# The fifteen multiplications of attention output by broadcast reciprocals, on GpSimd instead of VectorE

## The chip, the cores and the metric

The kernel runs on one core of a Trainium2 chip. Its time is device microseconds of one execution. Three runs of the kernel before gave 645.48, 646.23 and 646.55 us; the median is 646.23 us.

## The reference

Two blocks read the same input x (1 x 2048 x 512, bf16) and are mixed by a gate:

```
g = sigmoid((x * gate_w).sum(-1, keepdims=True))
qkv = x @ wqkv                       # 32 heads of 16
p = softmax(q @ k^T * 16 ** -0.5)
a = (p @ v) @ wo
b = ((x @ w_gate) * (x @ w_up)) @ w_down      # F = 1376
out = g * a + (1 - g) * b
```

## The kernel before, in words

**Tiling.** The 2048 queries are cut into four chunks of 512 (`cq`). The attention runs in 32 steps `m` (`NG`), eight for each chunk; a step covers four heads, one in each 32-row group of TensorE. Two steps, p = 0 and p = 1, make a pair `cb = m // 2` of eight heads, and a pair's result fills block `b` of the attention output OT of its chunk, so there are sixteen pairs. For each step TensorE multiplies a head's keys and queries into a PSUM bank (scores, L910, 128 keys x 512 queries, four heads side by side), and later exponentials and values into one bank (L1143, bank `OB`, the value bank), where a column of ones beside the values sums the denominators.

**Exponentials.** Two engines make them out of the score banks. ScalarE takes most tiles with its exponential (L1008, one to three banks at a time). VectorE takes the others with an approximation (L1043): it adds a bias and writes 16-bit integers whose bits are read as fp16. GpSimd then adds two constants to those bits, four 16-bit numbers at a time as a 64-bit integer (L1093, INT64_ADD), which makes two shifted copies; TensorE multiplies all three into the values, the copies with values scaled to match (VS). Results lie in the 58 cells of PT.

**Normalising a pair.** When a step's products are done, VectorE copies the value bank to `oc` (L1240, fp32). The denominators of both steps go through a DMA to `dn`, VectorE takes reciprocals (L1231) and multiplies them by the gate (L1229), DMAs write them to DRAM (L1228) and read them back broadcast over partitions into `rb` (L1224), and four DMAs bring the odd heads' rows into place in `oc` (L1196). Then comes the instruction that the change moves: L1222 multiplies `oc` by `rb`, both 128 x 512 fp32 in SBUF, into OT (bf16). Fifteen of the sixteen pairs go this way; the last has a path of its own (L1213 and after L1246). The next pair's first copy into `oc` (L1240) and its load of `rb` wait for that product (`mult_done`), and so do the output projections that read the block (`ev_ot`, L427 and L433).

**Order.** The program is recorded before it is built. A planner (`_Clock`) plays the kernel through with booked durations and picks, for each engine, the next ready task; a string of digits (`ORDER`) settles its choices. Each pick is appended to one list, and `emit` deals that list out to the engines: an engine's instructions stand in the order of the list, and a wait on a semaphore is set for each dependency on another engine's result or a DMA. Every engine runs its own list strictly in order. `eng` says which engine an operation goes to; `stream` and `seq` say which count the waits use.

```
o = K.issue("pool", fn, [x[2] for x in us] + [d for z in zs for d in pt_rel[z]], 157.0 + 218.0 * n, 182.0 + 218.0 * n)
...
const("pool", "add0", lambda g: g.int64_add(dmy[:, :].bitcast(I64), dmy[:, :].bitcast(I64), 0), ["dmy", "wgz", "qz0"], 1500, 1500)
```

The first line books an add, two of which follow each VectorE exponential; the second is a dummy add at the start (L416, booked at 1500 ns) whose result nobody reads.

Beside the attention run the projections of q, k and v, the up, gate and down products of the second block and the output projections, as fillers on TensorE (L427), with VectorE taking their results out of PSUM (L489, L534, L555, L624, L651, L714).

## Time and profile before

| | |
|---|---|
| median of three runs | 646.23 us |
| profiled execution, time | 647.98 us |
| profiled execution, span of the core | 645.3 us |
| granted TensorE clock | 1.0 |
| TensorE busy | 638.4 us, 99% |
| ScalarE busy | 622.0 us, 96% |
| VectorE busy | 605.1 us, 94% |
| GpSimd busy | 554.1 us, 86% |

A row of the costliest groups reads: line, engine, operation, what it writes and reads, shapes, count, then busy time and the mean duration of one, then the engine's idle time ahead of them and what ended it. A row of the timeline reads: start, duration, engine, line, operation, count merged, and in brackets the idle time ahead and what ended it. DVE is VectorE, ACT ScalarE, POOL GpSimd, PE TensorE, PEld its weight loads, SP the engine that issues DMAs. A q behind an engine's name stands for its sequencer.

### The profile page before, as it was taken

Reading aid. Unit: us, or ns where it says so; the run is one execution under the profiler, and the core shown is the slowest. Engines: PE = TensorE matmul, PEld = TensorE weight load, DVE = VectorE, ACT = ScalarE, POOL = GpSimd, SP = SyncE. Lnnn points to the kernel's source line nnn. Section 1 sums busy time; section 2 is a strip of 40 time slices with the busy share of each in tenths; the row PEclk is TensorE's granted clock in tenths of the full one; section 3 lists DMA queues with packets and bytes.
Section 4 is the critical chain, followed back from the end, with each engine's and each line's share of the span. In section 5 each row is a group of like instructions: output and inputs, shape, how many; then the busy total and the mean of one; then the engine's idle time right before and its main releaser. Section 6 shows DMA issues by size and latency. Waiting matters only on the chain.

```text
span 645.3 us, 21200 instructions
## 1 busy us (share of the span) xinstructions
PE 638.4 (99%) x8733; PEld 192.2 (30%) x8733; DVE 605.1 (94%) x1021; ACT 622.0 (96%) x753; POOL 554.1 (86%) x1431
## 2 busy tenths in 40 slices
PE   8999999999999999999999999999999999999997
PEld 3332332232223222223322222332322222322233
DVE  6999999999999999999998999999998999999986
ACT  5899999999999999999999999999999999999993
POOL 2669899998998989898889999988898998899982
PEclk9999999999999999999999999999999999999999
DMA  7940101000010100101010010100001010000101
GB/s 151 266 120 16 66 10 40 2 16 24 4 35 10 40 14 16 32 1 35 5 30 16 16 40 11 31 8 12 27 6 40 19 35 3 8 24 1 28 20 35
DMA packets 28658, 21.15 MB, mean 33 GB/s; under 512 B 16488, under 2 KB 24396, under 8 KB 28560
## 3 DMA queue, kind: packets, MB, share of 16 engines
q1 hardware_dynamic: 27600, 19.26, 11.6%
q8 instruction: 68, 1.11, 0.7%
q10 hardware_dynamic: 960, 0.52, 0.3%
q14 instruction: 30, 0.25, 0.1%
HBM read 11.63 MB, written 2.37 MB: 22 GB/s over the span
## 4 chain that ended last, share of the span: by engine, by line
PE 88%; ACT 9%; DVE 1%; DMA 1%; issue 0%; SPq 0%
PE ps L1143 32%; PE ps L427 28%; PE ps L910 26%; ACT PT L1008 9%; PE ps L433 3%; DVE OT L1222 1%; DMA wq<-in_A_wqkv_dram 1%; DVE PT L1043 0%; PE ps L1254 0%; SPq L354 0%; DVE QE L714 0%; PE ps L1446 0%; DVE fl L1441 0%; DVE cb L1451 0%
## 5 line engine op out<-in xcount | busy, mean ns | idle before, releaser
L1008 ACT ACTIVATE PT<-ps 128x1024 bf16<-128x1024 f32 (+2 forms) x743 | 616.2, 1001 | 6.6 <-PE ps L910 5.8
L1093 POOL INT64_ADD PT<-PT x1420 | 551.2, 413 | 76.2 <-DVE PT L1043 67.6
L1043 DVE TENSOR_SCALAR PT<-ps 128x512 int16<-128x512 f32 x728 | 471.5, 683 | 26.9 <-PE ps L910 15.5
L910 PE MATMUL ps<-QE,KK 32*128 32x512 bf16 x2048 | 245.7, 384 | 0.6 <-DVE PT L1043 0.4
L1143 PE MATMUL ps<-PT,V 128*32 128x512 bf16 (+1 forms) x2048 | 232.5, 384 | 0.0
L1143 PE MATMUL ps<-PT,VS 128*32 128x512 f16 x1456 | 186.7, 383 | 0.0
L910 PEld LDWEIGHTS ps<-QE,KK 32*128 32x128 bf16 x2048 | 63.7, 91 | 231.1 <-ACT PT L1008 183.7
L1143 PEld LDWEIGHTS ps<-PT,V 128*32 128x32 bf16 x2048 | 57.7, 95 | 62.9 <-issue 49.4
L1143 PEld LDWEIGHTS ps<-PT,VS 128*32 128x32 bf16 x1456 | 45.6, 95 | 42.0 <-issue 26.8
L427 PE MATMUL ps<-xT,wg 128*32 128x512 bf16 x704 | 54.6, 383 | 0.7 <-DVE PT L1043 0.7
L427 PE MATMUL ps<-xT,wu 128*32 128x512 bf16 x704 | 54.1, 383 | 0.0
L427 PE MATMUL ps<-wd,wa 128*32 128x512 bf16 x704 | 51.6, 382 | 0.0
L624 DVE TENSOR_TENSOR usb<-ps,omg 128x512 bf16<-128x512 f32 x44 | 29.9, 680 | 0.2
L651 DVE TENSOR_TENSOR wa<-ps,usb 128x512 bf16<-128x512 f32 x44 | 29.9, 680 | 0.1
L433 PE MATMUL ps<-wo,OT 32*128 32x512 bf16 x60 | 23.1, 385 | 0.1
L1240 DVE COPY oc<-ps 128x512 f32<-128x512 f32 x31 | 21.1, 680 | 0.0
L427 PEld LDWEIGHTS ps<-wd,wa 128*32 128x32 bf16 x704 | 14.8, 95 | 19.5 <-issue 11.9
L427 PE MATMUL ps<-xT,wa 128*32 128x512 bf16 x272 | 20.2, 382 | 0.0
L427 PEld LDWEIGHTS ps<-xT,wg 128*32 128x32 bf16 x704 | 13.8, 95 | 19.5 <-issue 11.1
L427 PEld LDWEIGHTS ps<-xT,wu 128*32 128x32 bf16 x704 | 13.8, 95 | 18.9 <-issue 10.4
L427 PE MATMUL ps<-xT,wq 128*32 128x512 bf16 x256 | 18.5, 382 | 0.6 <-DMA wq<-in_A_wqkv_dram 0.6
L427 PE MATMUL ps<-wa,xT 128*32 128x512 bf16 x256 | 17.1, 381 | 0.0
(74 smaller groups left out, 145.4 us busy)
## 6 DMA issues: line engine op xcount, KB each, us to landing
rb<-rscr SPq DMA_DIRECT2D x16, 256.0 KB
QE<-Qr SPq DMA_DIRECT2D x120, 16.0 KB, 1.8
oc<-oc SPq DMA_DIRECT2D x60, 32.0 KB, 1.9
out_dram<-ost SPq DMA_DIRECT2D x12, 128.0 KB, 1.8
wu<-in_B_w_up_dram SPq DMA_DIRECT2D x1, 1376.0 KB, 7.2
wg<-in_B_w_gate_dram SPq DMA_DIRECT2D x1, 1376.0 KB, 11.5
wd<-in_B_w_down_dram SPq DMA_DIRECT2D x1, 1280.0 KB, 14.9
wa<-in_A_wqkv_dram SPq DMA_DIRECT2D x1, 512.0 KB, 6.1
```

What stands on the lines that cost most here:

```text
L427: r = pe.matmul(ps[32 * i : 32 * i + 32, bank, :], w, x_, start=s0, stop=s1, tile_position=(0, 32 * i), skip_group_check=True)
L433: return pe.matmul(ps[:, bank, :], lhs[32 * q : 32 * q + 32, :], rhs[32 * q : 32 * q + 32, :], start=s0, stop=s1, tile_position=(32 * q, 0 ...
L624: return v.tensor_tensor(usb[:, st["s"], :], ps[:, bank, :], omg[:, cf, :], ALU.mult)
L651: return v.tensor_tensor(hT[:, f, :], ps[:, bank, :], usb[:, u_at[cf, f][0], :], ALU.mult)
L910: return lambda pe: pe.matmul(ps[:, bank, :], KK[32 * j : 32 * j + 32, b, kt * 128 : (kt + 1) * 128], QE[32 * j : 32 * j + 32, p, b, :], s ...
L1008: o = K.issue("act", lambda a: a.activation(PT[:, cs, :], ps[:, bs, :], ACT.Exp, scale=math.log(2.0) / 1024.0), deps, 63.0 + 427.0 * n, 17 ...
L1043: o = K.issue("dve", lambda v: v.tensor_scalar(PT[:, y, :].bitcast(I16), ps[:, bank, :], BIAS16, 0.0, ALU.add, ALU.max), [dep] + pt_rel[y] ...
L1093: return g.int64_add(PT[:, zl, :].bitcast(I64), PT[:, sl, :].bitcast(I64), w)
L1143: return lambda pe: pe.matmul(ps[32 * it.j : 32 * it.j + 32, OB, :], lhs, it.rhs, start=s0, stop=s1, tile_position=(0, 32 * it.j), skip_gr ...
L1222: lambda v: v.tensor_tensor(OT[:, cq % 2, b, :], oc[:, 0, :], rb[:, :], ALU.mult), 760.0, 840.0, None, 1, begun=md)
L1240: K.task("dve", deps, lambda v: v.tensor_copy(oc[:, p, :], ps[:, OB, :]), 600.0, 690.0, done, 0)
```

## The change

When the planner has picked a pair's multiplication and booked it on VectorE, the recorded operation is relabelled: its engine and stream become GpSimd's, and the two counters are put right. The planner still books VectorE's time for it, so no other choice moves: the whole list keeps its order, and fifteen entries of it go to another engine.

```diff
                                     def md(o7):
+                                        P.nstream["dve"] -= 1
+                                        o7.eng = o7.stream = "pool"
+                                        P.nstream["pool"] = o7.seq = P.nstream["pool"] + 1
                                         for tt in range(4):
                                             ev_ot[cq, b, tt] = o7
                                         mult_done[cb] = o7
```

Lines behind the diff move down by three: L1222 becomes L1225, L1240 becomes L1243.

GpSimd's list at the first of the fifteen places, the change against before (a + is new; names are the tiles written and read, PT the exponentials' cells, OT the attention output, oc the copied value bank, rb the broadcast reciprocals; s_dve, s_pe, s_drb and s_dodd are the semaphores of VectorE, TensorE, the load of rb and the moves of odd rows):

```order
 L1093 ISA PT<-PT 128x256 [waits s_dve]
 L1093 ISA PT<-PT 128x256
+L1225 ISA
+L1225 TENSOR_TENSOR OT<-oc,rb 128x512 [waits s_drb,s_dodd]
+L1093 ISA
 L1093 ISA PT<-PT 128x256 [waits s_dve,s_pe]
 L1093 ISA PT<-PT 128x256
```

Three instructions have come in between two pairs of adds: the multiplication, and one without operands on either side of it. In the built program these two are PseudoReloadLibraryIndex, the first with library index 0, the second with 1. Before, the program holds a single one, with index 1, ahead of the dummy add of L416. The same three stand at all fifteen places.

VectorE's list at the same place, from the last exponentials ahead of the multiplication to the copy of the next step's value bank, before:

```order
L1043 TENSOR_SCALAR PT<-ps 128x512 [waits s_pe] x2
L1222 TENSOR_TENSOR OT<-oc,rb 128x512 [waits s_drb,s_dodd]
L1043 TENSOR_SCALAR PT<-ps 128x512 [waits s_pe]
L489 CAST KK<-ps 128x512 [waits s_pe]
L1043 TENSOR_SCALAR PT<-ps 128x512 [waits s_pe] x2
L1043 TENSOR_SCALAR PT<-ps 128x512
L1043 TENSOR_SCALAR PT<-ps 128x512 [waits s_pe]
L1240 COPY oc<-ps 128x512 [waits s_pe]
```

and after:

```order
L1043 TENSOR_SCALAR PT<-ps 128x512 [waits s_pe] x3
L489 CAST KK<-ps 128x512 [waits s_pe]
L1043 TENSOR_SCALAR PT<-ps 128x512 [waits s_pe] x2
L1043 TENSOR_SCALAR PT<-ps 128x512
L1043 TENSOR_SCALAR PT<-ps 128x512 [waits s_pe]
L1243 COPY oc<-ps 128x512 [waits s_pool,s_pe]
```

The multiplication and its two DMA waits are gone from VectorE, nothing else has changed places, and the copy at the end, which overwrites `oc`, has a wait for GpSimd in addition.

## The prediction

> **What bounds the kernel now.** I read the page first: shares of busy time, then the costliest groups.

> ```profile
> span 645.3 us, 21200 instructions
> ...
> PE 638.4 (99%) x8733; PEld 192.2 (30%) x8733; DVE 605.1 (94%) x1021; ACT 622.0 (96%) x753; POOL 554.1 (86%) x1431
> ...
> L1008 ACT ACTIVATE PT<-ps 128x1024 bf16<-128x1024 f32 (+2 forms) x743 | 616.2, 1001 | 6.6 <-PE ps L910 5.8
> L1093 POOL INT64_ADD PT<-PT x1420 | 551.2, 413 | 76.2 <-DVE PT L1043 67.6
> L1043 DVE TENSOR_SCALAR PT<-ps 128x512 int16<-128x512 f32 x728 | 471.5, 683 | 26.9 <-PE ps L910 15.5
> ```

> ScalarE's exponentials alone fill 616 of 645 us, with 6.6 us of idle time ahead of them. TensorE waits for the score banks that they empty (the waits, below). VectorE and GpSimd form a second chain: VectorE writes an approximate exponential (L1043), GpSimd makes two shifted copies of it (L1093), TensorE multiplies all three into the values. That chain has little room left. The stretch from the first to the last multiplication, and its waits:

> ```profile
> core 0: us, PE busy (x) PEld busy (x) DVE busy (x) ACT busy (x) POOL busy (x), PEclk, DMA share, GB/s
> 76.00:612.00 536.00, 534.51 (x7280) 156.05 (x7280) 512.34 (x833) 533.70 (x634) 484.94 (x1249) 1.00 0.07 19
> ```

> ```profile
> PEld ps L910 <- ACT PT L1008: 183.7, 439, 0.5
> ...
> PEld ps L1143 <- POOL PT L1093: 7.3, 32, 0.2
> ```

> ACT is idle for 536.00 - 533.70 = 2.3 us there, and GpSimd for 536.00 - 484.94 = 51.1 us. These two numbers decide: VectorE time that is set free can shorten the kernel by hardly more than the 2.3 us, and GpSimd can take on about 51 us more, or 3.4 us for each of fifteen steps, before it sets the pace itself. Tensor work waits for an add only 32 times and never over 0.2 us: the adds now come early.

> **Part 1: what leaves VectorE.**

> ```profile
> L1222 DVE TENSOR_TENSOR OT<-oc,rb x15: 672/727/1906, 77.2 to 609.6; 128x512 bf16<-128x512 f32 x15
> ```

> ```profile
> L1222 DVE TENSOR_TENSOR OT<-oc,rb 128x512 bf16<-128x512 f32 x15 | 14.3, 951 | 0.0
> ```

> Fifteen instructions of 0.67 to 1.91 us, 14.3 us together, leave VectorE. Three are near 1.8 us, and here is what happens at one of them (VectorE, GpSimd, ScalarE):

> ```profile
> 148.77 1.91 POOL L1093 INT64_ADD PT<-PT  x5
> ...
> 149.32 1.91 DVE L1222 TENSOR_TENSOR OT<-oc,rb 128x512 bf16<-128x512 f32 x1
> ...
> 151.15 0.68 DVE L1043 TENSOR_SCALAR PT<-ps 128x512 int16<-128x512 f32 x1
> ...
> 151.93 0.77 POOL L1093 INT64_ADD PT<-PT  x2 [1.24 <-DVE PT L1043]
> ...
> 152.91 1.02 ACT L1008 ACTIVATE PT<-ps 128x1024 bf16<-128x1024 f32 x1 [0.72 <-PE ps L910]
> ```

> The multiplication ends 0.55 us after GpSimd's run of adds does (151.23 against 150.68): it could not get through while the adds ran back to back. ScalarE then stands for 0.72 us. The other two long ones cost it 0.40 and 0.18 us:

> ```profile
> 227.92 1.02 ACT L1008 ACTIVATE PT<-ps 128x1024 bf16<-128x1024 f32 x1 [0.40 <-PE ps L910]
> ```

> ```profile
> 536.37 1.02 ACT L1008 ACTIVATE PT<-ps 128x1024 bf16<-128x1024 f32 x1 [0.18 <-PE ps L910]
> ```

> Moving the multiplication ends these, since VectorE's work next to it reads PSUM: a gain of 0.72 + 0.40 + 0.18 = 1.3 us on the path. The rest of the 14.3 us is covered by ScalarE, which is busy all the while. Where the multiplication goes through at once, an add beside it stretches, as at the second one:

> ```profile
> L1093 POOL INT64_ADD PT<-PT x5: 394/402/830, 110.9 to 112.9; - x5
> ```

> That gives GpSimd back 0.83 - 0.40 = 0.4 us a time.

> **Part 2: what comes to GpSimd.** The order shows three new instructions at each of the fifteen places: a reload of GpSimd's instruction library (the program's PseudoReloadLibraryIndex, 0), the multiplication, and a second reload (1) ahead of the next add. The diff does not say so; adds and multiplication belong to different libraries. All three stand in line with the adds, so nothing of them is hidden except by GpSimd's own idle time.

> The multiplication itself: no two-input GpSimd operation stands in the trace. Bounds are the fill below, 1.38 us for 1536 numbers, so 0.46 us for 512, and four times an add of 0.40 us (an add reads 256 words, the multiplication 1024), 1.6 us. I take the middle, 1.0 us; the ends move the total by 15 x 0.6 = 9 us at most.

> The reload: the trace has one, ahead of the dummy add that the program makes early on.

> ```profile
> 4.14 1.38 POOL L415 MEMSET QE<- 128x1536 f32 x1 [2.19 <-DVE sel L406]
> 5.67 0.19 POOL L416 INT64_ADD dmy<-dmy  x1
> 13.33 0.78 POOL L1093 INT64_ADD PT<-PT  x2 [7.47 <-DVE PT L1043]
> ```

> ```profile
> L416 POOLq MODIFY_POOL_CONFIG  x2: 12/12/12, 5.5 to 5.6; - x2
> ```

> From the end of the fill (5.52) to the add (5.67) are 0.15 us: the lower end. The upper end is what GpSimd's idle time of 7.47 us behind it could have hidden, 7.5 us. Between them I have to choose. Nothing in the program before ever goes back to library 0, and the profiled execution is one of several of this program, so that one reload may have found its library already in place; after the change all thirty really switch. The planner also books 1500 ns for the dummy add, not the 192 ns that it took here. If code has to come from DRAM, the nearest rows are the single fetches of the start:

> ```profile
> wa<-in_A_wqkv_dram SPq DMA_DIRECT2D x1, 512.0 KB, 6.1
> ...
> wq<-in_A_wqkv_dram SPq DMA_DIRECT2D x1, 128.0 KB, 4.9
> ```

> I take the middle of these, 5.5 us, as an estimate. The sum for each place is 2 x 5.5 + 1.0 - 0.4 = 11.6 us, for fifteen 174 us; GpSimd's idle time takes up 51 of that, and 123 us are left. TensorE's early adds do not help for long: once it has used those made before a stall, each of its shifted products waits for GpSimd, scores stop, and ScalarE with them. The profiled execution took 648.0 us (a span of 645.3 and 2.7 around it), 1.7 more than the median of 646.2. From the median: 646.2 + 123 = 769 us; the 1.3 us of part 1 vanish in it.

> [...]

> **Part 3: waits that move.** VectorE loses its wait for the reciprocals' and the odd rows' DMAs (s_drb, s_dodd); GpSimd gets it, with all later adds behind it. It never held VectorE (idle 0.0 in the multiplication's row), and GpSimd reaches the place about when VectorE did, because an add follows its VectorE exponential closely. With 5.5 us of reload ahead, the data is there. VectorE's next copy out of the value bank (L1240, L1243 after) now waits for GpSimd; behind it are queued VectorE's exponentials, and TensorE waits for the bank:

> ```profile
> 77.19 0.73 DVE L1222 TENSOR_TENSOR OT<-oc,rb 128x512 bf16<-128x512 f32 x1
> ...
> 81.86 0.68 DVE L1240 COPY oc<-ps 128x512 f32<-128x512 f32 x1
> ```

> The copy starts 3.9 us after the multiplication's end. With 5.5 + 1.0 us on GpSimd against 0.73 it would stand for about 2 us, but inside the 11.6 us that the adds are held anyway, so I add nothing; with a cheap reload it costs nothing. The other reader is the output projection. At one place it follows at once:

> ```profile
> 492.51 0.68 DVE L1222 TENSOR_TENSOR OT<-oc,rb 128x512 bf16<-128x512 f32 x1
> ...
> 493.63 0.39 PE L427 MATMUL ps<-wo,OT 128*32 128x512 bf16 x4
> ```

> There TensorE, 0.4 us behind the product, waits from the first reload on, about 1 us if the reload is free and 6 us as forecast, again inside the 11.6. rb is loaded again a head pair later, and SP's order stays as it is: both at nothing.

> **Rivals.**

> *The reload finds both libraries in place* (not slower): then it is worth the 0.15 us of the dummy's row, fifteen places cost 15 x (0.3 + 1.0 - 0.4) = 13.5 us of 51 idle ones, and the three gains of 1.3 us remain, less what late adds and that one projection cost. 646.2 - 1.3 = 644.9 at best; if one place in three has no room and loses 0.9 us, 649. I say 645.5. For it: the row. It decides as long as 15 x (2c + 0.6) stays below 51 us, so for a reload c up to 1.4 us. Against it: that row needs no switch to have happened. Chance 0.31: 0.10 faster, 0.16 the same, 0.05 slower.

> *The reload costs about what ScalarE's table load does.*

> ```profile
> L386 ACT ACT_TABLE_LOAD x1 | 1.3, 1283 | 2.2 <-issue 2.2
> ```

> With 1.28 us, fifteen places cost 15 x 3.16 = 47 us, just under the 51 idle ones on average; but each is a block of 3.2 us, and places with less room let TensorE stand for part of it, at most about 20 us altogether: 650 to 665 us. Chance 0.12, slower.

> *VectorE is the bound and the reload is free*: its 14.3 us all come off, 632 us. Against it: ACT's 2.3 us of idle time. Chance 0.02, faster.

> **How the numbers follow.** My forecast, the reload as a fetch, has 0.55 and is the likeliest: 769 us, all of it slower. Its own range runs from 3.0 us a reload, 15 x 6.6 - 51 = 48 us, 694 us, to 7.5 us, 15 x 15.6 - 51 = 183 us, 829 us. A fast reload holds 0.33, too much to leave out, so the range starts at 645 and is cut at 815, leaving out the best cases below and the dearest above, some 15 in 100. A measurement of this kernel can tell a change of about 0.2%, 1.3 us. Faster: 0.10 + 0.02 = 0.12; the same: 0.16; slower: 0.55 + 0.12 + 0.05 = 0.72.

> **What would show it.** In the changed profile: thirty more library rows on GpSimd, and behind each a gap or a long first instruction of about 5.5 us; the multiplication at about 1.0 us; adds without the 0.8 us ones; ACT with idle time behind TensorE in fifteen places 38 us apart, and TensorE's value products waiting for GpSimd in long waits instead of 0.2 us. I am wrong if the adds follow the reload within 0.5 us and GpSimd's busy share only rises to some 88%; then the time stays within 3 us of before. I am wrong about the idle time if the reload is as forecast but much less than 51 us, or more, is given back.

## The result and the profile after

The median after is 836.52 us (six runs, 833.63 to 838.91), against 646.35 us for six runs of the kernel before on the same chip: a ratio of 1.2947, interval 1.293 to 1.2965, or 190 us more. (The ratios in this document can differ from the quotient of the two medians by up to 0.0008.) The direction was as forecast. The size was not: 769 us was the forecast, and 815 the end of the range.

The profiled execution took 836.67 us. From its page, the same lines as the prediction shows of the kernel before, and the moved multiplication's row:

```profile
span 833.6 us, 21266 instructions
...
PE 690.1 (83%) x8733; PEld 197.4 (24%) x8733; DVE 598.9 (72%) x1006; ACT 629.2 (75%) x753; POOL 564.5 (68%) x1446
...
L1008 ACT ACTIVATE PT<-ps 128x1024 bf16<-128x1024 f32 (+2 forms) x743 | 623.4, 978 | 187.6 <-PE ps L910 186.0
L1093 POOL INT64_ADD PT<-PT x1420 | 542.7, 400 | 148.3 <-DVE PT L1043 74.0
L1043 DVE TENSOR_SCALAR PT<-ps 128x512 int16<-128x512 f32 x728 | 474.2, 685 | 140.3 <-PE ps L910 130.1
...
L1225 POOL TENSOR_TENSOR OT<-oc,rb 128x512 bf16<-128x512 f32 x15 | 18.8, 1252 | 105.9 <-issue 99.0
```

The loss can be read off ScalarE: its exponentials' idle time has gone from 6.6 to 187.6 us, 181.0 more, and their busy time from 616.2 to 623.4, 7.2 more. Together that is 188.2 us, and the span has grown by 833.6 - 645.3 = 188.3 us. GpSimd's busy share has fallen from 86 to 68%: no engine is full any more. The waits, sorted by size:

```profile
ACT PT L1008 <- PE ps L910: 186.0, 67, 13.9
PEld ps L910 <- ACT PT L1008: 170.2, 396, 0.8
DVE PT L1043 <- PE ps L910: 130.1, 123, 14.2
PEld ps L1143 <- POOL PT L1093: 127.7, 84, 13.1
POOL OT L1225 <- issue: 99.0, 14, 7.6
PE ps L1143 <- POOL PT L1093: 96.9, 18, 12.8
...
POOL PT L1093 <- issue: 64.5, 11, 6.0
...
DVE oc L1243 <- POOL OT L1225: 26.8, 7, 6.1
```

TensorE's value products now wait for an add for up to 13.1 us, where the longest such wait was 0.2 us. GpSimd itself waits for nothing that has a name ("issue"): 99.0 / 14 = 7.1 us ahead of a multiplication, 64.5 / 11 = 5.9 us ahead of the next add. These are the two reloads. In the instruction list they are hardly to be seen: the sequencer's rows of one source line last 1 to 13 ns each, with a median of 11.

```profile
L1225 POOLq MODIFY_POOL_CONFIG  x30: 1/11/13, 77.7 to 783.0; - x30
```

The first of the fifteen places, GpSimd's timeline and then ScalarE's:

```profile
76.95 0.77 POOL L1093 INT64_ADD PT<-PT  x2 [0.29 <-DVE PT L1043]
84.67 1.25 POOL L1225 TENSOR_TENSOR OT<-oc,rb 128x512 bf16<-128x512 f32 x1 [6.95 <-issue]
91.98 32.14 POOL L1093 INT64_ADD PT<-PT  x86 [6.06 <-PE ps L910]
```

```profile
69.28 15.19 ACT L1008 ACTIVATE PT<-ps 128x1024 bf16<-128x1024 f32 x16
88.01 1.02 ACT L1008 ACTIVATE PT<-ps 128x1024 bf16<-128x1024 f32 x1 [3.54 <-PE ps L910]
89.96 2.08 ACT L1008 ACTIVATE PT<-ps 128x512 bf16<-128x512 f32 x3 [0.92 <-PE ps L910]
94.04 1.02 ACT L1008 ACTIVATE PT<-ps 128x1024 bf16<-128x1024 f32 x1 [2.01 <-PE ps L910]
```

No add is made from 77.72 to 91.98 us, a block of 14.3 us. ScalarE works on for 6.8 us, to 84.47, then stands for more than half of the time until the block's end, and again behind it. Over the fifteen places GpSimd's mean idle time is 105.9 / 15 = 7.06 us ahead of a multiplication and 5.86 us behind it, so a block is 7.06 + 1.25 + 5.86 = 14.17 us. The loss, 190.2 / 15 = 12.7 us for each place, is nearly all of it.

### The profile page after: what moved, and what is told of

Its sections match the earlier page's. It is cut to its first block, busy times and chain, and to the rows that moved or that the text cites. A ratio compares the mean times of both kernels' runs of the same rounds, so it can differ in the third digit from the quotient of the medians.

```text
span 833.6 us, 21266 instructions
## 1 busy us (share of the span) xinstructions
PE 690.1 (83%) x8733; PEld 197.4 (24%) x8733; DVE 598.9 (72%) x1006; ACT 629.2 (75%) x753; POOL 564.5 (68%) x1446
## 2 busy tenths in 40 slices
DMA packets 28659, 21.16 MB, mean 25 GB/s; under 512 B 16488, under 2 KB 24396, under 8 KB 28560
## 4 chain that ended last, share of the span: by engine, by line
PE 52%; POOL 20%; issue 19%; DVE 8%; DMA 1%; SPq 0%; POOLq 0%; DVEq 0%
PE ps L1143 18%; POOL PT L1093 18%; PE ps L427 17%; PE ps L910 15%; DVE PT L1043 5%; POOL OT L1225 2%; PE ps L433 2%; DVE oc L1243 1%; DVE usb L624 1%; DMA wq<-in_A_wqkv_dram 1%; DVE rec L1232 0%; DVE wa L651 0%; DVE Qr L534 0%; DVE rec L1234 0%; DVE ost L714 0%
## 5 line engine op out<-in xcount | busy, mean ns | idle before, releaser
L1008 ACT ACTIVATE PT<-ps 128x1024 bf16<-128x1024 f32 (+2 forms) x743 | 623.4, 978 | 187.6 <-PE ps L910 186.0
L1093 POOL INT64_ADD PT<-PT x1420 | 542.7, 400 | 148.3 <-DVE PT L1043 74.0
L1043 DVE TENSOR_SCALAR PT<-ps 128x512 int16<-128x512 f32 x728 | 474.2, 685 | 140.3 <-PE ps L910 130.1
L1143 PE MATMUL ps<-PT,VS 128*32 128x512 f16 x1456 | 212.2, 399 | 99.2 <-POOL PT L1093 96.9
L1143 PE MATMUL ps<-PT,V 128*32 128x512 bf16 (+1 forms) x2048 | 244.0, 399 | 21.1 <-DVE oc L1243 21.1
L910 PE MATMUL ps<-QE,KK 32*128 32x512 bf16 x2048 | 253.8, 399 | 3.1 <-DVE PT L1043 3.0
L910 PEld LDWEIGHTS ps<-QE,KK 32*128 32x128 bf16 x2048 | 63.1, 91 | 241.2 <-ACT PT L1008 170.2
L1225 POOL TENSOR_TENSOR OT<-oc,rb 128x512 bf16<-128x512 f32 x15 | 18.8, 1252 | 105.9 <-issue 99.0
L1143 PEld LDWEIGHTS ps<-PT,VS 128*32 128x32 bf16 x1456 | 50.2, 95 | 164.4 <-POOL PT L1093 127.7
L1143 PEld LDWEIGHTS ps<-PT,V 128*32 128x32 bf16 x2048 | 59.0, 96 | 88.3 <-issue 53.5
L1243 DVE COPY oc<-ps 128x512 f32<-128x512 f32 x31 | 21.2, 685 | 63.8 <-PE ps L1143 37.0
L427 PE MATMUL ps<-xT,wu 128*32 128x512 bf16 x704 | 56.7, 400 | 1.7 <-DVE PT L1043 1.7
L427 PE MATMUL ps<-xT,wg 128*32 128x512 bf16 x704 | 57.4, 401 | 0.0
L427 PE MATMUL ps<-wd,wa 128*32 128x512 bf16 x704 | 55.9, 410 | 0.0
L427 PE MATMUL ps<-wo,OT 128*32 128x512 bf16 x196 | 17.1, 395 | 12.9 <-POOL OT L1225 12.9
L427 PE MATMUL ps<-xT,wa 128*32 128x512 bf16 x272 | 20.8, 392 | 0.0
L427 PEld LDWEIGHTS ps<-wd,wa 128*32 128x32 bf16 x704 | 15.3, 98 | 22.2 <-issue 15.2
L427 PEld LDWEIGHTS ps<-xT,wu 128*32 128x32 bf16 x704 | 14.2, 97 | 23.5 <-issue 13.0
L427 PEld LDWEIGHTS ps<-xT,wg 128*32 128x32 bf16 x704 | 14.3, 96 | 20.7 <-issue 14.1
## 6 DMA issues: line engine op xcount, KB each, us to landing
out_dram<-ost SPq DMA_DIRECT2D x12, 128.0 KB, 1.7
wg<-in_B_w_gate_dram SPq DMA_DIRECT2D x1, 1376.0 KB, 11.5
wa<-in_A_wqkv_dram SPq DMA_DIRECT2D x1, 512.0 KB, 6.2
```

The costliest lines, as they stand in the source:

```text
L427: r = pe.matmul(ps[32 * i : 32 * i + 32, bank, :], w, x_, start=s0, stop=s1, tile_position=(0, 32 * i), skip_group_check=True)
L910: return lambda pe: pe.matmul(ps[:, bank, :], KK[32 * j : 32 * j + 32, b, kt * 128 : (kt + 1) * 128], QE[32 * j : 32 * j + 32, p, b, :], s ...
L1008: o = K.issue("act", lambda a: a.activation(PT[:, cs, :], ps[:, bs, :], ACT.Exp, scale=math.log(2.0) / 1024.0), deps, 63.0 + 427.0 * n, 17 ...
L1043: o = K.issue("dve", lambda v: v.tensor_scalar(PT[:, y, :].bitcast(I16), ps[:, bank, :], BIAS16, 0.0, ALU.add, ALU.max), [dep] + pt_rel[y] ...
L1093: return g.int64_add(PT[:, zl, :].bitcast(I64), PT[:, sl, :].bitcast(I64), w)
L1143: return lambda pe: pe.matmul(ps[32 * it.j : 32 * it.j + 32, OB, :], lhs, it.rhs, start=s0, stop=s1, tile_position=(0, 32 * it.j), skip_gr ...
```

## The experiments

Three theories were set against each other. **S**, a stall: a block of GpSimd's line is lost except for the one or two microseconds that early adds cover at that place, and idle time of GpSimd elsewhere gives nothing back. **W**, work: GpSimd's total decides, and its 51 us of idle time come off, as in the prediction. **R**: the loss lies in the multiplication on GpSimd and the waits that moved with it, not in the reloads. Each kernel is compared with the kernel before run on the same chip.

**The reloads without the multiplication.** The multiplication stays on VectorE; GpSimd makes a product of one number per partition at each place. The diffs of this section show the main edit alone; the lines that make a tile or fill it are left out.

```diff
+P.op("pool", lambda g: g.tensor_tensor(tny[:, 0:1], tny[:, 1:2], tny[:, 1:2], ALU.mult), [c["dmy"]])
```

> The product stays on VectorE; on GpSimd, at the same fifteen places, stands a multiplication of one number per partition, which belongs to library 0 and so brings the two reloads along. Theory S (each place is a block of the adds; what the early adds don't cover reaches ScalarE, which has no room to make it good): the block is 7.05 + 5.87 for the reloads and about 0.4 around a tiny product, 13.3 us against 14.25 in the change; the change lost 190 / 15 = 12.7 a place, 1.6 less than its block, so here 11.7 a place, 646 + 176 = 822 us. Theory W (GpSimd's total work sets the time and its 51 us of idle time come off, as the prediction had it): 15 x 13.3 - 51 = 149, 795 us. Rival R (the loss comes from the product itself on GpSimd, 1.25 us, and from the copy and the projections that wait for it): most of the loss is gone, under 700 us.

Measured: 826.77 us, ratio 1.2777 (1.2715 to 1.2838). GpSimd's timeline at the first place:

```profile
76.92 0.77 POOL L1094 INT64_ADD PT<-PT  x2 [0.29 <-DVE PT L1044]
85.15 0.18 POOL L1219 TENSOR_TENSOR tny<-tny 128x1 f32<-128x1 f32 x1 [7.46 <-DVE PT L1044]
91.18 1.89 POOL L1094 INT64_ADD PT<-PT  x5 [5.85 <-issue]
```

From 77.69 to 91.18 us no add is made: 13.5 us, 0.18 of it an instruction; the mean of the fifteen places is 13.25 us. The tiny product waits for no DMA, and GpSimd still stands for 7.19 us on average ahead of it, so the DMA waits that moved to the multiplication do not make its gap. 180 us of loss, with no multiplication moved and no wait moved: R falls as the main cause. W is 32 us off, S 5 us.

**Five places, and one.** The relabelling is kept where `cb % 3 == 1` (five of fifteen), and in a second kernel where `cb == 7`.

```diff
-P.nstream["dve"] -= 1
-o7.eng = o7.stream = "pool"
-P.nstream["pool"] = o7.seq = P.nstream["pool"] + 1
+if cb % 3 == 1:
+    P.nstream["dve"] -= 1
+    o7.eng = o7.stream = "pool"
+    P.nstream["pool"] = o7.seq = P.nstream["pool"] + 1
```

> Only every third pair's product moves (five of fifteen, 115 us apart before). Theory S: each costs what it cost in the change, 5 x 12.7 = 63, 710 us. Theory W: 5 x (12.9 + 1.25 - 0.4) = 69 us of work on GpSimd, of which its 51 us of idle time take up most: 664 us. Rival R: a third of the loss, as S.

> Only one product moves, that of pair 7. Theory S: one block, 12.7 us, 659 us, though more than 270 us of work with idle time on GpSimd follow it. Theory W: 13.8 us of work are taken up by that idle time, 646 us, at most 2 us more. In between means that a stall is partly made good.

Measured: five places 718.42 us (1.1099, 1.108 to 1.1118), 71.5 us more or 14.3 for each; one place 658.71 us (1.0181, 1.0167 to 1.0195), 11.8 us more. This tells S and W apart most plainly: five blocks, 14.5 us each by the trace, are 73 us, of which W would have taken 51 off, and one block would have vanished in them. Nothing of the kind happened. S was within 1 us for the single place and 8 us short for the five, which lost nearly the whole of their blocks. The single block, GpSimd's timeline and then ScalarE's:

```profile
336.86 4.53 POOL L1093 INT64_ADD PT<-PT  x12 [0.60 <-DVE PT L1043]
348.34 1.25 POOL L1226 TENSOR_TENSOR OT<-oc,rb 128x512 bf16<-128x512 f32 x1 [6.95 <-issue]
355.37 1.90 POOL L1093 INT64_ADD PT<-PT  x5 [5.78 <-DVE PT L1043]
```

```profile
333.18 11.87 ACT L1008 ACTIVATE PT<-ps 128x1024 bf16<-128x1024 f32 x14
350.85 1.02 ACT L1008 ACTIVATE PT<-ps 128x1024 bf16<-128x1024 f32 x1 [5.81 <-PE ps L910]
352.37 1.02 ACT L1008 ACTIVATE PT<-ps 128x1024 bf16<-128x1024 f32 x1 [0.49 <-PE ps L910]
353.89 1.02 ACT L1008 ACTIVATE PT<-ps 128x1024 bf16<-128x1024 f32 x1 [0.50 <-PE ps L910]
358.19 1.02 ACT L1008 ACTIVATE PT<-ps 128x1024 bf16<-128x1024 f32 x1 [3.28 <-PE ps L910]
359.70 1.94 ACT L1008 ACTIVATE PT<-ps 128x1024 bf16<-128x1024 f32 x2 [0.49 <-PE ps L910]
```

The block lasts from 341.39 to 355.37, 13.98 us. ScalarE works until 345.05 and makes three more tiles, so it stands for 5.81 + 0.49 + 0.50 us and part of the 3.28 inside the block; but after the block's end it stands for another 2.8 us and 0.49. TensorE's first stall here, 5.50 us from 344.14, ends with the moved product, which an output projection reads (its row stands below, under part 3); an add holds TensorE only from 354.38, for 1.44 us more. The windows around it show the clock that TensorE had:

```profile
345.00:350.00 5.00, 0.36 (x4) 0.11 (x4) 0.00 (x0) 0.04 (x1) 1.25 (x1) 0.58 0.00 0
350.00:355.00 5.00, 4.38 (x32) 0.70 (x28) 3.09 (x5) 3.07 (x3) 0.00 (x0) 0.50 0.10 30
355.00:360.00 5.00, 4.18 (x33) 0.90 (x33) 1.76 (x4) 1.32 (x2) 4.63 (x13) 0.55 0.00 0
360.00:365.00 5.00, 5.00 (x72) 1.31 (x68) 3.85 (x6) 5.00 (x6) 5.00 (x14) 1.00 0.01 2
```

The granted clock (the third number from the end) has dropped to 0.50 in the stall and is back at 1.00 only from 360 us: 33 matmuls in 5 us, against 72. If it steps straight between 1.00 and 0.50, then by the means of these windows and of windows of 2 us (0.96 from 344 to 346, 0.62 from 358 to 360) it drops at about 345.85, 1.7 us into the stall, and is back at about 359.50, 3.7 us after the matmuls resume for good. TensorE's burst from 349.64 to 354.38, 4.7 us, does not bring it back: from 350 to 355 the clock is 0.50. So early adds may cover more than the small difference of block and loss suggests, and a part may be taken back while TensorE restarts slowly; no run separates the two.

**A reload that really switches.** To see what the dummy add's reload costs when the other library is in place, the kernel before gets one tiny product as GpSimd's last instruction, so that the next execution starts from there.

```diff
+P.op("pool", lambda g: g.tensor_tensor(tny[:, 0:1], tny[:, 1:2], tny[:, 1:2], ALU.mult), [c["dmy"]])
```

> The kernel before with one tiny product of library 0 as GpSimd's last operation, so that an execution ends with library 0 in place. If the dummy add's reload was cheap because the execution before had left library 1 in place, the dummy add now starts about 5.9 us later than at 5.67, near 11.5 us, and the kernel takes the same time as before, 646 us, since the first add that anybody needs comes at 13.3. If something else puts library 1 in place, or a reload at the start is cheap by itself, the dummy add stays at 5.7.

Measured: 647.32 against 646.95 us (1.0001, 0.9992 to 1.001), the same. GpSimd's timeline at the start and at the end:

```profile
4.14 1.38 POOL L416 MEMSET QE<- 128x1536 f32 x1 [2.19 <-DVE sel L407]
11.32 0.18 POOL L417 INT64_ADD dmy<-dmy  x1 [5.79 <-issue]
...
639.68 0.18 POOL L1500 TENSOR_TENSOR tny<-tny 128x1 f32<-128x1 f32 x1 [6.73 <-issue]
```

The dummy add, which started 0.15 us after the fill in the kernel before, now starts 5.79 us after it, with the same instructions ahead of it. So the 0.15 us was that of a library left in place by the execution before. Here the reload is hidden, since no add is wanted until 13 us.

**What VectorE's time is worth.** Two kernels take the multiplication off VectorE without a reload. One, an edit of the kernel after, leaves it out and lets GpSimd copy half a block from `rb` and half from `oc` in its place; the other, an edit of the kernel before, cuts it to 8 of 512 columns on VectorE.

```diff
-v.tensor_tensor(OT[:, cq % 2, b, :], oc[:, 0, :], rb[:, :], ALU.mult)
+(v.tensor_copy(OT[:, cq % 2, b, 0:256], rb[:, 0:256]), v.tensor_copy(OT[:, cq % 2, b, 256:512], oc[:, 0, 256:512]))[-1]
```

```diff
-v.tensor_tensor(OT[:, cq % 2, b, :], oc[:, 0, :], rb[:, :], ALU.mult)
+v.tensor_tensor(OT[:, cq % 2, b, 0:8], oc[:, 0, 0:8], rb[:, 0:8], ALU.mult)
```

> The change without its reloads: in place of the product GpSimd copies half a block from rb and half from oc into OT, which needs no other library, with the same waits and readers. Left out is the multiplication itself. Theory S: the block is only the two copies, about 1 us, inside the 2 us of room that the run with one moved product showed, so nothing of the 190 us is left, and of the 1.3 us that the clash of VectorE's product with the adds cost ScalarE most comes off: 645 to 647 us beside 646.9. If the move itself hurts (VectorE's copy and the projections waiting for GpSimd): 650 us or more.

> The kernel before with VectorE's product cut to 8 of 512 columns; the rest of OT is left at zeros that GpSimd writes at the start. It bounds what freeing VectorE can bring. By the prediction's part 1 the gain is ScalarE's 1.3 us, so 645 to 646 us beside 646.9; if VectorE were the bound (the rival of 632 us), 15 products less would bring up to 13 us.

Measured: the copies 646.37 us (1.0001, 0.9992 to 1.001), the cut 646.03 us (1.0, 0.9991 to 1.0009), against 646.03 us. GpSimd's timeline at one place of the copies, and ScalarE's row of the cut kernel:

```profile
150.43 0.42 POOL L1225 CAST OT<-rb 128x256 bf16<-128x256 f32 x1
150.77 0.42 POOL L1225 CAST OT<-oc 128x256 bf16<-128x256 f32 x1
151.16 3.05 POOL L1093 INT64_ADD PT<-PT  x8
```

```profile
L1008 ACT ACTIVATE PT<-ps 128x1024 bf16<-128x1024 f32 (+2 forms) x743 | 615.5, 1008 | 5.1 <-PE ps L910 4.5
```

The casts follow the adds and the adds follow the casts with no gap: no reload. ScalarE's idle time falls by 1.5 us, about the 1.3 us that the prediction counted, and the three waits that it named are gone from the cut kernel's trace, but neither median shows it, within 0.1%. Freeing VectorE of this work wins nothing that the times show.

**Blocks of other lengths, without reloads.** The kernel before gets small fills in a chain on GpSimd at the fifteen places: 9, 18 or 52 of them.

```diff
+w_ = []
+for _ in range(9):
+    w_ = [P.op("pool", lambda g: g.memset(pad[:, :], 0.0), w_)]
```

> The kernel before, with a chain of nine small fills on GpSimd at each of the fifteen places, each waiting for the one before, about 3 us in all; no reload, the product stays on VectorE. Theory S with a room of about 2 us a place (a moved single product lost 11.8 of a block of 14.0): 15 x 1 = 15 us lost, 662 us. Theory W: 45 us of work go into 51 us of idle time, 647 us.

> The same with eighteen fills, about 6 us a place. Theory S: 15 x (6 - 2) = 60 us lost, 707 us. Theory W: 90 - 51 = 39 us, 686 us. Both are to be worked out again with the block that the trace shows.

> The kernel before with 52 small fills at each of the fifteen places, 52 x 0.254 = 13.2 us by the spacing of the eighteen, the length of the block that the two reloads and a tiny product made (13.3 us, 12.0 us lost a place). Theory S: a block is a block, no matter what fills it: 12 us a place, 646 + 180 = 826 us. Rival L (reloads do harm beyond the time that GpSimd stands, for instance to DMAs or to other engines): clearly less than 820 us, down to 646 + 15 x 13.2 - 51 = 793 us.

GpSimd's timeline at the first place, one row of each kernel:

```profile
77.89 2.31 POOL L1221 MEMSET pad<- 128x128 f32 x9
```

```profile
77.88 4.66 POOL L1221 MEMSET pad<- 128x128 f32 x18
```

```profile
77.57 13.56 POOL L1221 MEMSET pad<- 128x128 f32 x52
```

The times, with the others beside them (a block is the mean time in which GpSimd makes no add at a place, the loss the medians' difference over the number of places):

| kernel | time, us | ratio and interval | block, us | loss per place, us |
|---|---|---|---|---|
| copies | 646.37 | 1.0001 (0.9992 to 1.001) | 0.7 | 0 |
| 9 fills | 654.14 | 1.0125 (1.0109 to 1.014) | 2.2 | 0.5 |
| 18 fills | 684.77 | 1.0592 (1.0575 to 1.0608) | 4.6 | 2.6 |
| 52 fills | 829.46 | 1.2836 (1.2815 to 1.2857) | 13.5 | 12.2 |
| reloads alone | 826.77 | 1.2777 (1.2715 to 1.2838) | 13.2 | 12.0 |
| the change | 836.52 | 1.2947 (1.293 to 1.2965) | 14.2 | 12.7 |

The times on record for the 9 and 18 fills missed: they took the fills for longer than they are, 3 and 6 us, and W's 686 us for the 18 lies close to the 684.77 measured only for that reason. With the traced lengths W fails: for the 18 fills 15 x 4.66 = 70 us of work less 51 would leave 19, and 38.7 us were lost; the 9 fills, 35 us and thus inside the idle time, should have been free and cost 8.1 us. S, with its 2 us of room at each place, gives 15 x (4.58 - 2) = 39 and 15 x (2.23 - 2) = 3.5 us: right for the 18, 5 us short for the 9. For the 52 fills S said 826 us, and 829.46 came. They answer another rival, that a reload harms by more than its time, by a traffic that it makes or the like: the fills, in blocks of 13.47 us, lose 1.2 us less than their block, the reloads, in blocks of 13.25, 1.3 less, the change 1.5 less. Blocks of this length cost the same whatever they are made of.

## Why the prediction was right in direction and too low

*What bounds the kernel*: right in that VectorE is not the bound, as the two kernels that free it show. That ScalarE alone is, no run shows: TensorE was busy for 534.51 of the same 536.00 us. Wrong is that GpSimd could take on 51 us "before it sets the pace itself". GpSimd was not full after the change either; its 36 us of other idle time remained (730.0 - 499.94 = 230.1 us idle in the stretch, less 15 x 12.92 for the reloads):

```profile
76.00:806.00 730.00, 591.92 (x7365) 162.96 (x7358) 511.25 (x826) 546.78 (x642) 499.94 (x1276) 0.89 0.05 14
```

*Part 1*: the three waits of 1.3 us are real in the profile (the cut kernel has none of them, and its idle time is 1.5 us lower) and too small for the medians. What VectorE reads out of PSUM beside the adds shows no such hold before the change either: its 728 exponentials took 622 to 696 ns each, with GpSimd busy for 86% of the span.

*Part 2, the reload*: the argument was right, that the dummy's 0.15 us was no switch, and the tiny product at the end shows it. The size was too low: 5.5 us taken from DMA rows, 7.06 and 5.86 us measured. That it came this near is luck as far as the runs show: the recorded DMA queues have 28659 packets and 21.16 MB after, 28658 and 21.15 MB before, so thirty switches left no fetch in them that could be priced by a DMA row. *The multiplication*: 1.0 us taken, 1.25 measured, inside its bounds of 0.46 and 1.6. *The adds*: 0.4 us a place was forecast, and 551.2 - 542.7 = 8.5 us, 0.57 a place, came. Not all of it is due to the move: with 52 fills, where the product stays on VectorE, the adds take 5.3 us less as well. With these sizes the sum of 174 us becomes 15 x 14.17 - 8.5 = 204 us: 30 us of the miss.

*Part 2, the subtraction, the step that failed*: "GpSimd's idle time takes up 51 of that". Of 204 us the kernel lost 190, so 14 were given back, not 51: 37 us of the miss, and the larger part. With the right sizes and that step the forecast would have been 646.2 + 204 - 51 = 799 us; without the subtraction at all it is 850, and the 14 us that were measured in its place bring it to 836. The prediction set down the sign of this itself, "wrong about the idle time if" much less than 51 us is given back, and it had the reason at hand in its next sentence: early adds do not help for long. An engine's idle time over a stretch can be set against added work only if the engines behind it can run ahead by as much as the added work is long. Here they run ahead by a few microseconds, and what ScalarE, busy for 533.70 of the 536.00 us before, and TensorE have lost can't be made good later: they have no idle time to catch up in. That is why one block loses 11.8 of 13.98 us with 51 us of GpSimd's idle time around it.

*Part 3*: right. VectorE's copy waited 3.7 us at the first place, where 2 were forecast:

```profile
86.03 0.69 DVE L1243 COPY oc<-ps 128x512 f32<-128x512 f32 x1 [3.73 <-POOL OT L1225]
```

At the pair of the single block TensorE's output projection waited 5.5 us for the product where 6 were forecast:

```profile
349.64 0.62 PE L427 MATMUL ps<-wo,OT 128*32 128x512 bf16 x4 [5.50 <-POOL OT L1226]
```

Both lie inside the block, and since 52 fills that nobody waits for lose about as much of their length, they add nothing that the times show.

*The rivals*: both libraries in place falls with the measured gaps. The table-load size falls too, but its remark that places with less room lose "at most about 20 us altogether" in blocks of 3.2 us fits the fills: between 8.1 us at 2.2 and 38.7 us at 4.6, a straight line gives some 21 us at 3.2. That remark contradicted the subtraction in the main sum. VectorE as the bound falls with the two kernels that free it.

*Left open*: how much of each loss is the slow restart at half clock, and what a switch does in its 6 to 7 us. In the kernel with one block 3.3 of ScalarE's 10.2 us of added idle time (16.8 against 6.6) come after the adds have resumed, and how much of that would come at full clock too was not measured. No kernel was made that keeps the clock up through a block. Places differ: the single one, pair 7, is among the five. If losses add up, the other four lost (71.5 - 11.8) / 4 = 14.9 us each, a little more than their blocks of 14.6 us. TensorE ran on for 2.1 to 5.0 us in these four and then stood in one piece for 10.0 to 13.1 us, against 5.7 and 1.5 us at pair 7. So block less lead is a guide to the loss and not a law, and what the restart adds was not measured.

## What to carry to other kernels

Idle time of an engine is not a store that added work can draw on: cost a block on the path by its length less the lead that the engines behind it have at that place, place by place, and expect up to the whole length where they stand long (11.8 of 13.98 us at the single place here, 71.5 of 73 at the five). Before an operation moves to GpSimd, look in the built program for library reloads, and price both directions (7.06 and 5.86 us here). A reload in a profile of repeated executions says nothing on the price of a switch unless the library before it was another one: the same dummy add came after 0.15 us and after 5.79.
